# Two fused attention and MLP layers on one core: the opening and the last two tiles rebuilt

## The chip, the core and the metric

The kernel runs on one core of a Trainium2 chip. The metric is the device time of one execution in microseconds (us). Before the change it is 1752.79 us, the median of three runs (1751.76 to 1753.04). The core's engines are named as in the profile: PE (TensorE, matmuls; PEld its weight loads), DVE (VectorE), ACT (ScalarE), POOL (GpSimd) and SP (SyncE, which issues DMAs here). They run side by side, each through its own list of instructions in order, and wait for each other by semaphores.

## The reference

Two times the same pair of layers on 2048 tokens of 512 channels, in bf16, with the same weights in both passes:

```python
def A(x, wqkv, wo):                       # 32 heads of 16 channels
    q, k, v = split(x @ wqkv)
    p = softmax(einsum("bhqd,bhkd->bhqk", q, k) * 16 ** -0.5)
    return merge(einsum("bhqk,bhkd->bhqd", p, v)) @ wo
def B(x, w1, w2):                         # 512 -> 1792 -> 512
    return silu(x @ w1) @ w2
x = x + A(layernorm(x)); x = x + B(layernorm(x))
x = x + A(layernorm(x)); x = x + B(layernorm(x))
```

With 32 heads and 2048 x 2048 scores in each of two layers, the exponentials are the bulk of what has to be done.

## The kernel before, in words

**Tiles.** The 2048 tokens are 16 tiles of 128. A head has 16 channels, so four heads lie side by side in the 128 partitions of a K tile (the `KT` tiles hold keys, transposed, with every other group of 16 partitions set to constants). A *block* is a group of four heads against one chunk of queries: 512 queries, or 256 for the last two chunks of a layer. A *unit* is 512 columns of scores of one head: 128 keys by 512 queries, or two times 128 keys by 256 queries.

**The stream.** `stream` goes through the blocks of both layers. In each step `emit_s` lets PE compute three or two units of scores into one of two PSUM slots (`s3`, 128x1536, and `s2`, 128x1024, in turn), and ACT takes the exp of the whole slot into `p`. Where DVE has room, `spare` gives one more unit to it: it is computed in one of three PSUM banks `g`, and `exp_on_dve` does its exp as a chain of four DVE operations (`v`, then `e` three times). PE then multiplies `p` or `e` by the values (`emit_pv`). A block's sum is copied out of PSUM to `oT`, transposed, and divided by its row sums (`finish_seq`): the transpose is a DMA on SP for most blocks and one on PE for the last two blocks of all (`bank=b in blocks[-2:]`).

**Fill.** All other matmuls (keys, queries, values, projection by `wo`, the two MLP products) are cut into steps of one matmul and put into lanes. `fill_step` puts them into the gaps between scores. `dummy` adds matmuls without use where the planner expects PE to be busy for less than 66% of 3.42 us.

**Who sets the order.** The order is made at build time by a planner in the kernel, `Machine`. It keeps an estimated duration for each instruction and the time at which each engine comes free, tracks which operation reads and writes which stretch of which tile (`span`, `track`), and issues each engine's pending operation that is ready first (`choice`, `pump`); among those, a lower `prio` goes first, and on DVE an operation of `prio` -1 is waited for by up to 0.16 us. PE's order is the order in which `stream` calls it. So every instruction of the listing is recorded at one of a few helper lines: L256 (`Engine.op`, all ACT and DVE operations), L395 (`mm`), L399 (`transpose`), L611 (`by_dma`), L1682 (the dummy exp that loads its table).

**The opening.** After the loads, `x` is normalized (tiles 3 and 7 by sums on ACT, the others by `bn_stats` on DVE), the first eight tiles are scaled into `room` (the `p` tiles), transposed on PE, copied to `xt`, and from these come keys, queries and values of the first block. Along with the first statistics ACT makes eight small constants (`minus`, `extra`, `sel`, 128x4 each), then three groups of roots (`y`), then the dummy exp. A K step (`k_seq`) takes the maximum of |k| (`amaxp`, DVE) and writes two `KT` tiles, one on ACT and one on DVE while nothing streams. A Q step (`q_seq`) makes |q| (`qa`, a DVE operation with a bit mask), a matrix `E` from the maxima and `minus` and `extra`, one matmul `qa` x `E` on top of the queries, and a copy to `qt`. While `before` has work, `order` returns its lanes as `(prep, firsts, turns)` and then `values`.

**The tail.** The last chunk of layer 2 is two tiles. When no scores wait any more, `stream` calls `last` three times: part 0 transposes three quarters of the attention output on PE, and parts 1 and 2 multiply each tile by `wo` into the free score slots, on top of `x` (added by a product with the identity). `end_tokens` then transposes the last quarter, adds its product, runs eight matmuls `warm` without use, copies the two sums to `x_sb` (one on ACT, one on DVE), takes their statistics, makes the reciprocal roots with three Newton steps on DVE for each tile, scales, transposes, runs three more `warm`, then the MLP: 56 matmuls with `w1`, tanh on ACT and a multiply on DVE, 28 matmuls with `w2`, and the sum to `out`.

Of the kernel before, what the change touches and what calls it, by code (L numbers as in the profile page):

```python
# [21 lines left out]
class Op:  # L22
    __slots__ = ("eng", "pitch", "tail", "deps", "end", "fn", "prio")
    __hash__ = object.__hash__

    def __init__(self, eng, pitch, tail, deps, fn, prio):
        self.eng, self.pitch, self.tail, self.deps = eng, pitch, tail, deps
        self.fn, self.prio, self.end = fn, prio, None


class Machine:
# [10 lines left out]
    WINDOW = 3.42  # L42

# [9 lines left out]
    def span(self, ap):  # L53
        key = (ap.name, ap.offset, ap.ap, ap.dtype)
        got = self.cache.get(key)
        if got is None:
            step = ap.ap[0][0]
            lo = ap.offset - ap.start_partition() * step
            hi = lo + 1 + sum(s * (n - 1) for s, n in ap.ap[1:] if s > 0)
            size = BYTES[ap.dtype]  # L60
            g = self.grain.get(ap.name, 1)
            got = self.cache[key] = (lo * size // g, -(-hi * size // g))
        return got

    def track(self, op, reads, writes):
        deps = {}
        for ap in reads:
            lo, hi = self.span(ap)
            known = self.regions.setdefault(ap.name, {})
            for (a, b), (w, _) in known.items():  # L70
                if a < hi and lo < b and w is not None:
                    deps[w] = 1
            mine = known.setdefault((lo, hi), [None, []])
            if op.eng == "PE":
                mine[1][:] = [o for o in mine[1] if o.eng != "PE"]
            mine[1].append(op)
        for ap in writes:
            lo, hi = self.span(ap)
            known = self.regions.setdefault(ap.name, {})
            for (a, b), (w, rs) in list(known.items()):  # L80
                if a < hi and lo < b:
                    if w is not None:
                        deps[w] = 1
                    deps.update(dict.fromkeys(rs))
                    if lo <= a and b <= hi:
                        del known[a, b]
            known[lo, hi] = [op, []]
        deps.pop(op, None)
        return deps

    def written(self, *aps):

        t = 0.0
        for ap in aps:
            lo, hi = self.span(ap)
            for (a, b), (w, _) in self.regions.get(ap.name, {}).items():
                if a < hi and lo < b and w is not None and w.eng != "PE":
# [5 lines left out]
    def released(self, ap):  # L103

        t = 0.0
        lo, hi = self.span(ap)
        for (a, b), (w, rs) in self.regions.get(ap.name, {}).items():
            if a >= hi or lo >= b:
                continue
# [52 lines left out]
    def choice(self, eng):  # L162
# [8 lines left out]
        wait = {-1: 0.16, 0: 0.1} if eng == "DVE" else {}  # L171
# [5 lines left out]

    def pump(self, until):
        while True:
            at, eng = min((self.choice(e)[0], e) for e in self.pending)  # L180
            if at > until:
                return
            at, op = self.choice(eng)
# [138 lines left out]
def kernel(  # L322
# [109 lines left out]
    def best_bank():  # L432
        return min(range(len(banks) if opening[0] else 3), key=bank_time)

    def take_bank():
        i = best_bank()
# [63 lines left out]
    for par in range(2):  # L500
        for out_, i, w in (
            (minus[par][:], 1, 1),
            (extra[par][:], 0, 1),
            (sel[:, par, 0:4], 0, 0),
            (sel[:, par, 4:8], 0, 2),
        ):
            A.activation(
                out_, blk[:], ACT.Identity, scale=cols[:, 2 * par + i, w : w + 1]
            )


# [36 lines left out]
    def ln_stats(mvb, i, tt, **kw):  # L548
        st = st_ring.turn()
        V.bn_stats(st[:], x_sb[:, tt, :], **kw)  # L550
# [137 lines left out]
    def q_seq(L, c, pr, early=False, which=(0, 1), when=None):  # L688
# [3 lines left out]
        def step(ct):  # L692
            def fn(g):
                if ct == 0:
                    box["QT"] = [qt_ring.take() for _ in which]
                    box["E"] = [e_turn[i].turn() for i in range(len(which))]
                    if c == 0:
# [3 lines left out]
                            out=amax[pr][:], in_=amaxp[pr][:, 0:n], axis=AX.X, op=ALU.max  # L701
# [9 lines left out]
                if ct == 0:  # L711
                    for i, par in enumerate(which):
                        V.scalar_tensor_tensor(
                            out=box["E"][i][:, 16 - 16 * par : 128 : 32], in0=minus[par][:],
                            scalar=amax[pr][:, 0:1], in1=extra[par][:], op0=ALU.mult, op1=ALU.add,
                        )
                    if len(which) > 1:
                        V.tensor_scalar_mul(
                            out=box["E"][1][:, 16:128:32], in0=box["E"][0][:, 16:128:32],
                            scalar1=-1.0,  # L720
                        )
                if ct < CT - 1:
                    return
                V.tensor_scalar(
                    out=qa[:].bitcast(U16),
                    in0=g[:, :].bitcast(U16).rearrange("p (n h) -> p n h", h=2)[:, :, 1],
                    scalar1=0x7FFF, scalar2=None, op0=ALU.bitwise_and,
                )
# [56 lines left out]
    def epilogue_seqs(L, c):  # L785
# [12 lines left out]
        def project(i):  # L798
            def step(ct):
                def fn(g):  # L800
# [11 lines left out]
                    ln_stats(box["mvb"], i, tts[i])  # L812
# [14 lines left out]
    def ffn_seqs(L, nxt, c, ln_box):  # L827
# [51 lines left out]
        def down(i):  # L879
            def step(ft):  # L880
                def fn(g):
# [15 lines left out]
                    else:  # L897
                        ln_stats(box["mvb"], i, tts[i])
# [55 lines left out]
    def end_projection(L, box, part, g):  # L954

        attn = L.attn[L.nch - 1]

        aT2 = KT[0][:, 0:1024].rearrange("p (i a b) -> p i a b", i=2, a=CT)  # L960
        if part == 0:
            b = take_bank()
            t_ps = as_bf16(banks[b])[:, 0 : 6 * P].rearrange("p (i a b) -> p i a b", i=2, a=3)
            for i in range(2):
                for ct in range(3):
                    transpose(t_ps[:, i, ct, :], attn[:, i, ct * P : (ct + 1) * P], ident[:, :])
            for i in range(2):
                V.tensor_copy(out=aT2[:, i, 0:3, :], in_=t_ps[:, i])
            give_bank(b)
            box["aT"], box["x"] = aT2, []  # L970
            return
        i = part - 1
        x_ps = s_slots[(g + part) % 2][:, 0, :]
        box["x"].append(x_ps)
        mm(x_ps, lhsT=ident[:, :], rhs=x_sb[:, tiles_of(L, L.nch - 1)[i], :], start=True, stop=False)
        for ct in range(3):
            mm(x_ps, lhsT=aT2[:, i, ct, :], rhs=wo_sb[:, ct, :], start=False, stop=False)

    def end_tokens(L, box, g):

        attn = L.attn[L.nch - 1]
        tts = tiles_of(L, L.nch - 1)
        b = take_bank()
        t_ps = as_bf16(banks[b])[:, 0 : 2 * P].rearrange("p (a b) -> p a b", a=2)
# [3 lines left out]
        give_bank(b)  # L988
        for i in range(2):
            mm(  # L990
                box["x"][i], lhsT=box["aT"][:, i, 3, :], rhs=wo_sb[:, 3, :],
# [8 lines left out]
        for i in (1, 0):  # L1000
            ln_stats(mvb, i, tts[i])
        a, y, ah, t = (keep([P, 2], FP32, f"end{k}") for k in ("a", "y", "h", "t"))
        V.tensor_scalar_add(
            out=a[:].rearrange("p (n o) -> p n o", o=1), in0=mvb[:, 0:2, 1:2], scalar1=float(EPS)
        )
        V.tensor_scalar(
            out=y[:].bitcast(I32), in0=a[:].bitcast(I32), scalar1=-0.5, scalar2=float(0x5F3759DF),
            op0=ALU.mult, op1=ALU.add,
        )
        V.tensor_scalar_mul(out=ah[:], in0=a[:], scalar1=-0.5)  # L1010
        one = [slice(0, 1), slice(1, 2)]
        for _ in range(3):
            for i in one:
                V.scalar_tensor_tensor(
                    out=t[:, i], in0=y[:, i], scalar=ah[:, i], in1=y[:, i],
                    op0=ALU.mult, op1=ALU.mult,
                )
            for i in one:
                V.scalar_tensor_tensor(
                    out=y[:, i], in0=t[:, i], scalar=1.5, in1=y[:, i], op0=ALU.add, op1=ALU.mult  # L1020
                )
        xnT = at_ring.take()[:, :, 0:256]
        for i in range(2):
            V.tensor_scalar(
                out=hT[:, i, :], in0=x_sb[:, tts[i], :], scalar1=mvb[:, i, 0:1], scalar2=y[:, one[i]],
                op0=ALU.subtract, op1=ALU.mult,
            )
        gs = [i for i in range(3) if i != b]
        for i in range(2):
# [3 lines left out]
            dst = xnT[:, :, i * P : (i + 1) * P]  # L1033
# [79 lines left out]
    def stream(layers, before, values, side, last, second_half):  # L1113
# [120 lines left out]
        def emit_s(tp):  # L1234
            g = made[0]
            if not started[0]:
                started[0] = True
                second_half()
# [37 lines left out]
        def finish_seq(b):  # L1276
# [3 lines left out]
            def fn(g):  # L1280
                if c not in L.attn and b.part != "early":
                    L.attn[c] = at_ring.take()
                if g is None:
# [49 lines left out]
                [(fn, b.w, lambda: [oT[:]])], bank=b in blocks[-2:],  # L1333
                when=lambda: b.part == "early" or c in L.attn or at_ring.room(),
            )

        def block_done(b):
# [14 lines left out]
            L.ready[c] = L.ready.get(c, 0) + 1  # L1352
            if L.ready[c] == HB and (c < L.nch - 1 or L.nxt is not None):
# [45 lines left out]
        def step_of(lane, tp, ready=True):  # L1399
# [5 lines left out]
            if s.at == 0:  # L1405
# [4 lines left out]
                if s.bank and bank_time(best_bank()) > (tp + 0.02 if ready else 1e12):  # L1410
# [7 lines left out]
        def do_step(lane):  # L1418
            s = lane.seqs[0]
            if s.at == 0:  # L1420
                if s.lock:
                    Lane.locks.add(s.lock)
                if s.bank:
                    s.own = take_bank()
# [145 lines left out]
        part = 0  # L1570
        while True:
# [13 lines left out]
            if not waiting:  # L1585
                g = made[0] - 1
                if part == 0 and bank_time(best_bank()) <= tp:
                    last(0, g)
                    part = 1
                    continue  # L1590
                if part in (1, 2) and M.released(s_slots[(g + part) % 2][:]) <= tp:
                    last(part, g)
# [203 lines left out]
```

## Time and profile before

| what | us |
|---|---|
| median of three runs | 1752.79 |
| the profiled execution, its own time | 1754.26 |
| its span, from the first instruction to the last event | 1752.4 |
| first exp starts | 22.32 |
| last exp ends | 1722.85 |
| hidden matmuls of the last two tiles start (chain) | 1735.62 |
| waits of ACT between first and last exp, 17 in all | 10.5 |
| exps on ACT: 1536 columns, 1024 columns | 722, 723 |
| exp chains on DVE | 484 |

The page's first part has each engine's busy time and its share of the span. A timeline row has the start and the length in us, the engine, the line of the code, the operation, what it writes and reads and, in brackets, how long its engine was idle before it and for whom it waited. A row of waits has the total in us, the number of waits and the longest. The chain is followed back from the last instruction, each step to what released it.

### The profile page before, as it was taken

The page shows a single profiled execution, that of the slowest core. Times are in us where ns is not written, and L with a number is a line of the kernel's source. Part 1 is how long each engine was busy: PE and PEld are TensorE (multiplying, and loading weights), DVE is VectorE, ACT ScalarE, POOL GpSimd, SP SyncE. Part 2 cuts the span into 40 slices and gives each one's busy share as a digit, 9 for nine tenths or more (in the row PEclk, how much of TensorE's full clock was granted, in tenths as well). Part 3 has the DMA queues.
Part 4 walks back from the last instruction along what each step waited for, and adds up shares of the span by engine and source line. Part 5 has one row for each costly group of instructions (what it writes and reads, how often), then busy time and mean ns, then how long its engine had stood idle before and what let it go on. Part 6 is the DMA issues. An engine that isn't in the chain of part 4 may idle for free.

```text
span 1752.4 us, 32102 instructions
## 1 busy us (share of the span) xinstructions
PE 1532.9 (87%) x12537; PEld 533.0 (30%) x12750; DVE 1640.2 (94%) x3193; ACT 1708.9 (98%) x1604; POOL 6.6 (0%) x20
## 2 busy tenths in 40 slices
PE   8898888898889888898889888889888798888897
PEld 2222222222222223333423222222222222333344
DVE  8999999999989999899899985989999999998995
ACT  8999999999999999999999999999999999999994
POOL 1000000000000000000000000000000000000000
PEclk9998999999999999999999999999999999999999
DMA  5100001000010001000010000100001000110100
GB/s 183 34 10 7 13 19 19 4 19 7 19 16 7 16 7 33 4 16 19 9 23 7 16 7 19 31 7 16 7 16 23 4 19 4 20 18 6 32 12 7
DMA packets 96968, 33.14 MB, mean 19 GB/s; under 512 B 88368, under 2 KB 96304, under 8 KB 96816
## 3 DMA queue, kind: packets, MB, share of 16 engines
q1 hardware_dynamic: 96816, 31.09, 8.0%
q8 instruction: 99, 1.62, 0.4%
q14 instruction: 53, 0.43, 0.1%
HBM read 7.86 MB, written 2.10 MB: 6 GB/s over the span
## 4 chain that ended last, share of the span: by engine, by line
ACT 50%; issue 17%; DVE 16%; PE 14%; DMA 3%; SPq 0%; ACTq 0%; another core or an unknown queue 0%; DVEq 0%
ACT p L256 47%; PE g L395 9%; DVE e L256 6%; PE s L395 5%; DVE v L256 3%; ACT t_sb L256 3%; DMA o<-oT 2%; DVE hT L256 1%; DVE KT L256 1%; DVE amaxp L256 1%; DVE oT L256 0%; DVE qt L256 0%; DVE qa L256 0%; DVE x_sb L256 0%; DMA x_sb<-in_A_x_dram 0%
## 5 line engine op out<-in xcount | busy, mean ns | idle before, releaser
L256 ACT ACTIVATE p<-s 128x1536 bf16<-128x1536 f32 (+1 forms) x1445 | 1664.8, 1397 | 10.1 <-PE s L395 7.6
L395 PE MATMUL s<-qt,KT 32*128 32x512 bf16 (+1 forms) x4513 | 569.0, 338 | 136.0 <-ACT p L256 122.0
L395 PE MATMUL g<-p,vaug 128*32 128x512 bf16 (+1 forms) x4513 | 477.0, 344 | 14.8 <-ACT p L256 13.3
L395 PEld LDWEIGHTS <-KT 32*128 32x128 bf16 x5128 | 209.5, 91 | 651.6 <-issue 639.6
L256 DVE TENSOR_SCALAR v<-g 128x512 f32<-128x512 f32 x484 | 330.6, 683 | 23.1 <-PE g L395 18.0
L256 DVE SCALAR_TENSOR_TENSOR e<-e,v 128x512 uint16<-128x512 bf16 x484 | 327.7, 680 | 0.5
L256 DVE SCALAR_TENSOR_TENSOR e<-v,e 128x512 bf16<-128x512 uint16 x484 | 326.9, 680 | 0.6
L256 DVE SCALAR_TENSOR_TENSOR e<-v 128x512 bf16<-128x512 uint16 x484 | 324.8, 681 | 0.9
L395 PEld LDWEIGHTS <-vaug 128*32 128x32 bf16 x5120 | 139.7, 95 | 210.3 <-issue 197.9
L395 PE MATMUL g<-wo_sb,ident 128*128 128x512 bf16 x612 | 187.7, 384 | 10.7 <-issue 4.0
L395 PE MATMUL g<-qt,KT 32*128 32x512 bf16 (+1 forms) x607 | 187.3, 341 | 0.8 <-DVE hT L256 0.5
L395 PE MATMUL g<-e,vaug 128*32 128x512 bf16 (+1 forms) x607 | 175.8, 345 | 2.7 <-DVE e L256 1.3
L395 PE MATMUL g<-w_sb,hT 128*128 128x512 bf16 x404 | 119.8, 383 | 4.0 <-issue 3.2
L395 PE MATMUL g<-xt,w_sb 128*128 128x512 bf16 x303 | 95.1, 388 | 15.9 <-DVE hT L256 10.1
L256 DVE SCALAR_TENSOR_TENSOR hT<-t_sb,g 128x512 bf16<-128x512 f32 x105 | 71.6, 682 | 17.8 <-ACT t_sb L256 16.7
L395 PEld LDWEIGHTS <-ident 128*128 128x128 bf16 x712 | 54.3, 98 | 101.4 <-issue 81.2
L256 ACT ACTIVATE t_sb<-g 128x512 f32<-128x512 f32 x105 | 77.8, 741 | 0.9 <-PE g L395 0.5
L256 DVE CAST oT<-g 128x512 bf16<-128x512 f32 (+1 forms) x94 | 55.6, 591 | 12.8 <-PE g L395 12.5
L395 PEld LDWEIGHTS <-hT 128*128 128x128 bf16 x568 | 41.5, 97 | 79.9 <-issue 62.5
L395 PEld LDWEIGHTS <-w_sb 128*128 128x128 bf16 x560 | 44.4, 99 | 69.3 <-issue 58.4
L256 DVE CAST qt<-g 128x512 bf16<-128x512 f32 x78 | 53.1, 681 | 3.6 <-PE g L395 3.4
L395 PE MATMUL g<-xt,wq_sb 128*128 128x512 bf16 x141 | 45.1, 393 | 2.8 <-issue 1.9
(129 smaller groups left out, 627.1 us busy)
## 6 DMA issues: line engine op xcount, KB each, us to landing
w_sb<-in_B_w_dram SPq DMA_DIRECT2D x2, 1792.0 KB, 13.9
x_sb<-in_A_x_dram SPq DMA_DIRECT2D x4, 512.0 KB, 6.8
out_dram<-x_sb SPq DMA_DIRECT2D x7, 256.0 KB, 2.1
o<-oT SPq DMA_TRANSPOSE x92, 2.4
xt<-hT SPq DMA_TRANSPOSE x48, 2.4
wk_sb<-in_A_wqkv_dram SPq DMA_DIRECT2D x1, 512.0 KB, 6.0
wq_sb<-in_A_wqkv_dram SPq DMA_DIRECT2D x1, 512.0 KB, 7.0
wv_sb<-in_A_wqkv_dram SPq DMA_DIRECT2D x1, 512.0 KB, 7.9
```

Source lines behind the costliest of these rows:

```text
L256: return self.m.submit(self.name, pitch, tail, aps, outs, lambda: fn(*args, **kw), prio)
L395: lambda: nc.tensor.matmul(out, lhsT=lhsT, rhs=rhs, **kw),
```

## The change: what it does

Opening: the eight constants are submitted after the roots with `prio` 2, so they go where ACT has nothing else; the dummy exp goes behind the first |q|; |q| of the queries made before the first scores is ACT's `Abs` and no longer DVE's bit mask; maxima and `E` get `prio` -1 before the stream starts, and DVE waits up to 0.4 us for such operations until then; the lane of transposes stands ahead of that of keys and queries; a query step takes one of the three `g` banks only.

Stream: the planner tracks a strided tile as up to eight stretches (`spans`) in place of one (`span`), and of two operations at the same time it issues the one that was submitted first.

Tail: three quarters of the last attention output go through two DMA transposes, and the two tiles' first projections become two sequences of fill in the lane `main`, which may begin when `calm` holds (the next-to-last block is done, at most 18 units are left, no DVE chain is under way). They stay in two `g` banks. The next-to-last block's transpose is a DMA; the last block's is put into the slot `s2`. `end_tokens` first runs a dummy square root (table load), takes the statistics of both tiles from PSUM, copies both sums to `x_sb` on ACT, makes one root for both tiles on ACT and one reciprocal on DVE, then a dummy tanh (table load). Both transposed tiles are copied by DVE. `warm` runs eleven and one matmuls in place of eight and three.

The diff, cut to its core:

```diff
 class Machine:
+    WAIT = {-1: 0.16, 0: 0.1}
-    def span(self, ap):
+    def spans(self, ap):
...
+            dims = [(s, n) for s, n in ap.ap[1:] if s > 0 and n > 1]
+            starts = [lo]
+            while len(dims) > 1 and len(starts) * dims[0][1] <= 8:
...
     def pump(self, until):
         while True:
-            at, eng = min((self.choice(e)[0], e) for e in self.pending)
+            at, op = min((self.choice(e) for e in self.pending), key=self.first)
...
                         V.tensor_reduce(
-                            out=amax[pr][:], in_=amaxp[pr][:, 0:n], axis=AX.X, op=ALU.max
+                            out=amax[pr][:], in_=amaxp[pr][:, 0:n], axis=AX.X, op=ALU.max,
+                            prio=0 if started[0] else -1,
                         )
...
-                V.tensor_scalar(
-                    out=qa[:].bitcast(U16),
...
+                if not started[0]:
+                    A.activation(qa[:], g[:, :], ACT.Abs)
+                    if pr == 0:
+                        M.submit(
+                            "ACT", 1.5, 0.1, [qa[:]], [lnt[:, 0:1]],
+                            lambda: nc.scalar.activation(lnt[:, 0:1], onescol[0], ACT.Exp),
+                        )
+                else:
+                    V.tensor_scalar(
...
-    def end_projection(L, box, part, g):
+    def end_projection(L, box, calm):
+        for i in range(2):
+            by_dma(attn[:, i, 0 : 3 * P], aT[:, i, 0:3, :])
...
+            return Seq(
+                [(fn, 512, lambda: [aT[:, i, 0:3, :]]) for fn in steps], bank=False,
+                when=lambda: calm() and bank_time(best_bank()) <= M.now(),
+            )
...
-    def end_tokens(L, box, g):
+    def end_tokens(L, box):
+        first_use(ACT.Sqrt, onescol[0])
...
-        warm(8, idle[:, :])
-        A.copy(x_sb[:, tts[0], :], box["x"][0])
-        V.tensor_copy(out=x_sb[:, tts[1], :], in_=box["x"][1])
+        warm(11, idle[:, :])
...
+        for i in range(2):
+            M.force(V.bn_stats(sts[i][:], x_ps[i]))
+            M.force(A.copy(x_sb[:, tts[i], :], x_ps[i]))
+            give_bank(box["x"][i])
+        for i in range(2):
+            M.force(V.bn_aggr(mvb[:, i, :], sts[i][:]))
+        root, rstd = (keep([P, 2], FP32, n) for n in ("root", "rstd"))
+        A.activation(root[:], mvb[:, 0:2, 1], ACT.Sqrt, bias=eps[:, 0:1])
+        V.reciprocal(rstd[:], root[:])
+        first_use(ACT.Tanh, root[:, 0:1])
...
-            if i == 0:
-                V.tensor_copy(out=dst, in_=t_ps)
-            else:
-                A.copy(dst, t_ps)
-        warm(3, idle[:, :])
+            V.tensor_copy(out=xnT[:, :, i * P : (i + 1) * P], in_=t_ps)
+        warm(1, idle[:, :])
...
+                if b is blocks[-1]:
+                    g = s_slots[1][:, 0, :]
...
-                [(fn, b.w, lambda: [oT[:]])], bank=b in blocks[-2:],
+                [(fn, b.w, lambda: [oT[:]])], bank=False,
...
+        def calm():
+            b = blocks[-1]
+            return blocks[-2].done and sum(b.left) <= GU * DEFER and all(o.end is not None for o in chains)
...
+            if c == L.nch - 1 and L.nxt is None and L.ready[c] == HB - 2:
+                main.add(last(calm))
...
     M.free.update(ACT=4.0, DVE=2.5)
+    M.WAIT = M.WAIT | {-1: 0.4}
...
-        [L1, L2], (prep, firsts, turns), values, side,
-        lambda part, g: end_projection(L2, end_box, part, g), second_half,
+        [L1, L2], (prep, turns, firsts), values, side,
+        lambda calm: end_projection(L2, end_box, calm), second_half,
```

More of the change, by code (lines that the diff above doesn't have):

```diff
@@ L430, in bank_time, with best_bank, take_bank @@
         return INF if shut[i] else M.released(banks[i][:])
[L432 to L436, printed above, removed]
+    def best_bank(every=True):
+        return min(range(len(banks) if opening[0] and every else 3), key=bank_time)
+    def take_bank(every=True):
+        i = best_bank(every)
         assert not shut[i]
@@ L499 @@
     sel = keep([P, 2, 8], BF16, "sel")
[L500 to L509, printed above, removed]
     started = [False]
@@ L1679 @@
     )
[L1680 to L1683 removed]
+    for par in range(2):
+        for out_, i, w in (
+            (minus[par][:], 1, 1),
+            (extra[par][:], 0, 1),
+            (sel[:, par, 0:4], 0, 0),
+            (sel[:, par, 4:8], 0, 2),
+        ):
+            by = cols[:, 2 * par + i, w : w + 1]
+            M.submit(
+                "ACT", 0.12, 0.1, [y[:, 0:1]], [out_],
+                lambda out_=out_, by=by: nc.scalar.activation(out_, blk[:], ACT.Identity, scale=by),
+                prio=2,
+            )
     halves_asked = [True, False]
```

200 lines of the change are left out of this document (95 added, 105 removed).

## The prediction

> **What bounds the kernel now.** I read the engines and the chain first, then ScalarE's waits between the first and the last exp, then the timeline of both ends.
>
> ```profile
> PE 1532.9 (87%) x12537; PEld 533.0 (30%) x12750; DVE 1640.2 (94%) x3193; ACT 1708.9 (98%) x1604; POOL 6.6 (0%) x20
> ...
> ACT 50%; issue 17%; DVE 16%; PE 14%; DMA 3%; SPq 0%; ACTq 0%; another core or an unknown queue 0%; DVEq 0%
> ```
>
> ```profile
> ACT p L256 <- PE s L395: 7.6, 13, 0.9
> ACT p L256 <- PE g L395: 1.9, 4, 0.7
> ```
>
> ScalarE (ACT) bounds: its first exp starts at 22.32, its last ends at 1722.85, and in those 1700.5 us it waits only 10.5 (the five rows of that answer; its two largest are shown). So the time has three terms: 22.32 of opening, the stream (ACT's own work), and a tail of 1752.4 - 1722.85 = 29.55. VectorE's 94% is no bound in the stream: it takes what exps it has room for.
>
> ```profile
> 8.66 0.28 ACT L256 ACTIVATE minus<-blk,cols 128x4 f32<-128x4 f32 x1
> ...
> 10.93 1.28 ACT L1682 ACT_TABLE_LOAD   x1
> 10.94 0.20 DVE L256 RECIPROCAL y<-y 128x8 f32<-128x8 f32 x1 [1.96 <-ACT y L256]
> ...
> 11.96 0.83 PE L399 MATMUL x<-ident,p 128*128 128x128 bf16 x12
> ...
> 16.99 0.69 DVE L256 TENSOR_REDUCE amaxp<-g 128x1 f32<-128x512 f32 x1 [1.40 <-ACT KT L256]
> ...
> 18.91 0.68 DVE L256 TENSOR_SCALAR qa<-g 128x512 uint16<-128x512 uint16 x1
> ...
> 21.00 0.69 DVE L256 CAST qt<-g 128x512 bf16<-128x512 f32 x1 [0.27 <-PE g L395]
> ...
> 22.32 18.27 ACT L256 ACTIVATE p<-s 128x1536 bf16<-128x1536 f32 x16
> ```
>
> In the opening VectorE (DVE) sits 1.96 waiting for ACT's roots, and ACT is late because eight constants stand before them. From 16.99 to 21.69 DVE is busy without a gap worth naming, and the first exp follows its query copy by 22.32 - 21.00 = 1.32.
>
> ```profile
> 1723.48 0.40 PE L395 MATMUL g<-p,vaug 128*32 128x256 bf16 x4
> ...
> 1726.68 0.59 ACT L256 CAST x_sb<-s 128x512 bf16<-128x512 f32 x1 [3.83 <-PE s L395]
> ```
>
> ```profile
> 1735.62 7.25 PE s L395 x56
> 1742.86 0.05 issue
> 1742.91 6.00 PE g L395 x27
> ```
>
> In the tail (timeline, then the chain) every step waits for the one before: the last exp's values product starts 0.63 after it, behind projections, and the 56 hidden matmuls start at 1735.62, 12.77 after it. They take 7.25, because TensorE (PE) has half its clock from 1731 to 1737.8 (windows of 1 us).
>
> **The tail, from the last exp's end at 0.** The change puts both tiles' projections ahead of it as fill, so the product need not queue. Product at 0.06 (PE's usual step after another engine: 1733.67 to 1733.73), 0.40; copy of it 0.50 to 0.92 (0.42); two transposes from 0.98, 0.28; reciprocal 1.30, multiply 1.54 to 1.83, transposes 1.88, copy 2.21, projections 2.56, all at the spacings of the old rows from 1724.68 to 1726.26. First tile's sums 0.42 later, 2.98. DVE now takes statistics straight from PSUM: 2.98 to 3.67 and 3.69 to 4.38 (0.69 each; the reading from PSUM has no row, and I bound it by the same operation's 0.66 and a 512-column PSUM reduce's 0.69). ACT's two copies wait for these, as the order of the instructions shows, 3.70 and 4.41 to 5.00 (0.59). The root is queued behind the second copy: 5.0 to 5.28 (0.28, as the y rows of the opening), reciprocal 5.32 (0.20), two scalings from 5.55, 0.33 apart, transposes 6.02 and 6.54 (0.61), DVE's copies 6.66 and 7.18 to 7.60 (0.42). Hidden matmuls: 7.65 instead of 12.77. What went: 0.87 of queueing, a copy ahead of each statistic, seventeen small DVE operations from 1729.77 to 1733.26, and two of three warming matmuls at half clock (0.43 each). The root's table load (1.28) runs from 0 to 1.5, and the one for tanh from 5.3 to 6.8 with the first tanh due at 9.4: both hidden; beyond these covers each microsecond would count fully.
>
> At full clock the 56 take 6.1 instead of 7.25: 2.23 of the old run was at half clock, which leaves 45.5 matmuls in 5.01, 0.110 each. Then 6.0 down, 0.04, 0.69 and the 2.77 of output as before. The tail is 23.3, 6.25 less.
>
> **The clock takes some back.** In the new tail PE is idle 1.8 of the time from -0.2 to 2.56, as it has no dummies there. The old trace has windows of 3.41 us, with the clock halved in the next one after windows in which PE was 60 to 75% busy or less: six in the stream, but others at 58 to 65% passed. Counted back from the halving at 1730.98, a window that holds over 1.3 us of this idle time starts between -1.65 and 0.7, which is 2.35 of 3.41 positions, 0.7. Then the eleven warming matmuls (2.4) run partly at 0.43, and the transposes wait behind them on PE's queue: 0.5 to 1.05, I take 0.8. So **tail -5.45**.
>
> The Trainium skill (TensorE: Matmul & The Clock Gate, Part 1) has free-running windows of 3413 ns and half clock after at least one idle window. The trace agrees on the length (6.83 us of halving) and not on idle: a window 30% busy was enough. By the page's rule as it stands the tail would be -6.25 and the sum 1746.9.
>
> **The opening.** The constants leave the front of ACT's queue, eight at 0.19 (1.5 with their waits). Roots end at 9.53 instead of 10.91 and DVE's reciprocal starts at 9.56. But PE is in twenty dummies until 11.96 (0.427 each at half clock), so the transposes begin there as before: nothing gained yet. ACT's three copies of transposes run 12.38 to 14.03 (0.53 apart), and one key matmul then stands in PE's queue ahead of the last eight transposes: keys of half 0 end at 15.6 (16.14 before). ACT copies the last tile after four constants, 15.26 to 15.85, which hold it 0.3; keys of half 1 end at 16.9, queries at 17.8. DVE's maximum goes 15.64 to 16.33, ACT's KT 16.36 and 17.10 to 17.88, DVE's KT 17.17 to 17.97 and its second maximum to 18.62; |q| is on ACT, 17.9 to 18.5 (0.59, by the vaug cast), so DVE loses 0.68. amax and E follow, E on PE 19.06, but the second KT (0.80) now stands before the query copy: 20.0. First exp 21.3. The exp table's load, 18.5 to 20.0 with its first use, is under this. **Opening -1.0**, from 0 (the dummies still hold everything) to -2 (their clock rises earlier).
>
> The Trainium skill (ScalarE: Activation LUTs, What ACT_TABLE_LOAD costs) gives 2.66 us a switch, a drain included. Here the load at 10.93 takes 1.28 and its first function runs at 12.22, so no drain shows. By the page the vaug cast after the load would end at 22.0, the opening would win 0.3, and the sum would be 1748.4.
>
> **The stream.** Compared instruction by instruction, DVE does 481 exp chains instead of 484, and ACT one 1536-column exp more. Sixteen exps in 18.27 are 1.14 each; 1536 and 1024 columns differ by 1.609 - 1.186 = 0.42, so a long one is 1.35. **+1.35**. The rest of the order changes too, since the planner tracks strided tiles finely and breaks ties otherwise: ACT's 10.5 of waits may come out from 0 to double. I take no change, by the six half-clock windows there, which hold 4.2 of it (0.7 each): a few windows more or fewer, +-3, is the width. The two DMA transposes added on SP for the projection and the one instead of PE's transpose for the next-to-last block are issued many exps before their users (2.4 to land); no wait.
>
> Sum: -1.0 + 1.35 - 5.45 = -5.1. The profiled run took 1754.26 (span 1752.4 and 1.86 around), so 1749.2 against itself; it stands 1.47 above the median 1752.79, and from that: **1747.7**.
>
> **Rivals.** (1) No halving in the tail: -5.9, 1746.9. For it: the windows at 58 to 65% that passed. (2) The load of the exp table stands in the way, or the dummies do: -4.4, 1748.4. Against it: nothing waits for the load in my order for 1.2 us. (3) The reordered stream loses what the ends win: seven half-clock windows more at 0.7 are +4.9, 1752.6, no change. For it: the windows come where PE is just under its share, which a new order shifts at random. (4) Slower: PE waits in order for things that the planner thinks ready (its costs are written for it), scores queue behind, and ACT waits. An ACT wait costs 0.62 (10.5 over 17); slower by 0.2% needs 8.6, fourteen more among 1445 exps. At twenty more: +7.3, 1760. Against it: the old plan is followed within 17 waits.
>
> **How the numbers follow.** 0.2% is 3.5 us, about what a measurement of this kernel can tell. Forecast 0.42, (1) 0.18, (2) 0.08: faster 0.68; (3) 0.25, same; (4) 0.07, slower. The range goes from the forecast less 4 (no halving, opening -2, stream -2) to the centre of (3): 1743.7 to 1752.8.
>
> **What would show it.** First exp at 21.3; 723 long exps; ACT's waits in the stream near 10; a tail of about 24; hidden matmuls 8.4 after the last exp, at full clock; root right behind the second copy. The prediction is wrong if the stream's waits change by over 3, if the copies do not end before 5.1, or if PE stays at half clock into the hidden matmuls.

## The result and the profile after

Over 20 runs of each, the changed kernel takes 1749.51 us on the median and the kernel before 1754.36; the ratio is 0.9973 (95% interval 0.9962 to 0.9983), 4.7 us less. The profiled execution took 1750.5 (span 1748.7), against 1754.26 (span 1752.4). One run of the kernel before, beside the experiments, took 2166.7 us at a mean granted clock of 0.555; no figure below counts it.

| term | before | forecast | after | forecast of the difference | measured |
|---|---|---|---|---|---|
| first exp starts | 22.32 | 21.3 | 21.49 | -1.0 | -0.83 |
| stream, to the end of the last exp | 1700.53 | 1701.9 | 1703.18 | +1.35 | +2.65 |
| tail | 29.55 | 24.1 | 24.03 | -5.45 | -5.52 |
| span | 1752.4 | 1747.3 | 1748.7 | -5.1 | -3.7 |

The profile's engines and chain of the changed kernel, and ACT's waits from the first exp to the last:

```profile
PE 1575.7 (90%) x12733; PEld 533.1 (30%) x12733; DVE 1629.3 (93%) x3165; ACT 1713.8 (98%) x1610; POOL 6.6 (0%) x20
...
ACT 44%; DVE 21%; PE 16%; issue 15%; DMA 3%; ACTq 0%; DVEq 0%
```

```profile
ACT p L280 <- PE s L419: 7.7, 16, 0.9
ACT p L280 <- PE g L419: 3.1, 5, 1.5
```

ACT is the bound as before. The first of these two rows counts the wait of 0.94 that stands before the first exp and so belongs to the opening. Without it ACT's waits in the stream sum to 10.2 us, against 10.5, so the added 2.65 are no waits that a row shows: they are one long exp more (1.35) and 1.6 besides.

The opening's timeline:

```profile
9.37 0.20 DVE L280 RECIPROCAL y<-y 128x8 f32<-128x8 f32 x1 [0.39 <-ACT y L280]
...
11.79 0.83 PE L423 MATMUL x<-ident,p 128*128 128x128 bf16 x12
...
17.46 0.60 ACT L280 ACTIVATE qa<-g 128x512 bf16<-128x512 f32 x1
18.07 1.28 ACT L743 ACT_TABLE_LOAD   x1
...
19.67 0.68 DVE L280 CAST qt<-g 128x512 bf16<-128x512 f32 x1
...
21.00 0.39 PE L419 MATMUL s<-qt,KT 32*128 32x512 bf16 x3 [0.61 <-DVE vaug L280]
21.49 1.45 ACT L280 ACTIVATE p<-s 128x1536 bf16<-128x1536 f32 x1 [0.94 <-PE s L419]
```

DVE's reciprocal comes 1.57 earlier and waits 0.39 instead of 1.96, yet the first transposes stand where they stood, 11.79 against 11.96. The query copy ends at 20.35, but the first scores wait until 21.00 for another DVE operation, the copy of a values tile (`vaug`): it empties the opening's bank that the first score slot takes over.

The tail's:

```profile
1724.68 1.28 ACT L1014 ACT_TABLE_LOAD   x1
...
1727.93 1.29 DVE L280 BATCH_NORM_STATS2 st<-g 128x6 f32<-128x512 f32 x2 [0.70 <-PE g L419]
1728.12 3.79 PE L419 MATMUL g<-wo_sb,ident 128*128 128x512 bf16 x11
1728.67 1.18 ACT L280 CAST x_sb<-g 128x512 bf16<-128x512 f32 x2 [2.48 <-DVE st L280]
...
1729.74 0.30 ACT L280 ACTIVATE root<-mvb,eps 128x2 f32<-128x2 f32 x1
1730.06 1.28 ACT L1014 ACT_TABLE_LOAD   x1
...
1731.75 0.61 PE L423 MATMUL g<-ident,hT 128*128 128x128 bf16 x8
...
1732.98 6.27 PE L419 MATMUL s<-attn,w_sb 128*128 128x256 bf16 x56 [0.41 <-DVE attn L280]
```

The last exp ends at 1724.66. The root starts 5.08 later, straight behind the second copy, and the first scaled tile is there at about 6.0. The transposes start at 7.09, because eleven warming matmuls stand in front of them and take 3.79: the clock is at half from 1727.2 to 1730.6. The hidden matmuls start 8.32 after the last exp (before: 12.77 by the chain, 12.56 by their timeline row) and run at full clock.

### The profile page after: what moved, and what is told of

It is laid out like the page before. It is cut to its first block, busy times and chain, and to the rows that moved or that the text cites. A ratio compares the mean times of both kernels' runs of the same rounds, so it can differ in the third digit from the quotient of the medians.

```text
span 1748.7 us, 32237 instructions
## 1 busy us (share of the span) xinstructions
PE 1575.7 (90%) x12733; PEld 533.1 (30%) x12733; DVE 1629.3 (93%) x3165; ACT 1713.8 (98%) x1610; POOL 6.6 (0%) x20
## 4 chain that ended last, share of the span: by engine, by line
ACT 44%; DVE 21%; PE 16%; issue 15%; DMA 3%; ACTq 0%; DVEq 0%
ACT p L280 41%; PE g L419 10%; DVE e L280 9%; PE s L419 5%; DVE v L280 4%; ACT t_sb L280 3%; DMA o<-oT 3%; DVE KT L280 2%; DVE hT L280 1%; DVE qt L280 1%; DVE amaxp L280 1%; DVE oT L280 1%; DVE vaug L280 0%; DVE qa L280 0%; DVE attn L280 0%
## 5 line engine op out<-in xcount | busy, mean ns | idle before, releaser
L280 ACT ACTIVATE p<-s 128x1536 bf16<-128x1536 f32 (+1 forms) x1446 | 1671.1, 1410 | 11.7 <-PE s L419 7.7
L419 PE MATMUL g<-wo_sb,ident 128*128 128x512 bf16 x681 | 210.6, 385 | 7.8 <-DVE v L280 5.3
L419 PE MATMUL g<-w_sb,hT 128*128 128x512 bf16 x448 | 131.2, 384 | 0.9 <-DVE hT L280 0.8
L419 PE MATMUL g<-xt,w_sb 128*128 128x512 bf16 x336 | 100.2, 387 | 9.3 <-DVE hT L280 6.5
L280 ACT ACTIVATE t_sb<-g 128x512 f32<-128x512 f32 x105 | 82.4, 784 | 0.6 <-PE g L419 0.3
L419 PE MATMUL g<-xt,wq_sb 128*128 128x512 bf16 x160 | 50.4, 390 | 1.9 <-DVE v L280 0.9
```

What stands on the lines that cost most here:

```text
L280: return self.m.submit(self.name, pitch, tail, aps, outs, lambda: fn(*args, **kw), prio)
L419: lambda: nc.tensor.matmul(out, lhsT=lhsT, rhs=rhs, **kw),
```

## The experiments

My theory is that the three terms add: two ends that win, and a stream that loses through the planner's part. The main rival is that the terms depend on each other: that the fill or the work put off at the ends is paid for in the stream. The table gives one profiled execution of each kernel; "half" is the number of half-clock windows (3.41 us each) within the stream, and ACT's waits are those after the start of the first exp. A ratio is to the runs of before on the same chip, whose median was 1753.8 to 1755.0.

| kernel | median, ratio to before (95%) | first transposes, first exp | stream | long exps, chains | ACT's waits, half | tail |
|---|---|---|---|---|---|---|
| before | 1754.36 | 11.96, 22.32 | 1700.53 | 722, 484 | 10.5, 6 | 29.55 |
| changed | 1749.51, 0.9973 (0.9962 to 0.9983) | 11.79, 21.49 | 1703.18 | 723, 481 | 10.2, 5 | 24.03 |
| changed_again | 1750.53, 0.9983 (0.9970 to 0.9995) | 10.51, 20.21 | 1705.80 | 723, 481 | 13.2, 7 | 22.89 |
| planner_only | 1756.34, 1.0002 (0.9988 to 1.0016) | 12.29, 24.16 | 1701.40 | 723, 480 | 10.3, 3 | 29.04 |
| tail_only | 1751.96, 0.9990 (0.9977 to 1.0003) | 11.83, 23.65 | 1703.14 | 723, 480 | 11.6, 4 | 22.91 |
| open_only | 1760.50, 1.0026 (1.0010 to 1.0042) | 11.74, 21.44 | 1706.95 | 723, 481 | 13.5, 6 | 29.81 |
| old_planner | 1743.96, 0.9941 (0.9925 to 0.9956) | 10.62, 19.87 | 1700.00 | 722, 484 | 9.5, 9 | 23.03 |
| tail_alone | 1749.87, 0.9974 (0.9961 to 0.9988) | 11.85, 22.34 | 1704.66 | 722, 484 | 12.8, 8 | 24.20 |
| gaps_filled | 1749.47, 0.9980 (0.9968 to 0.9992) | 10.77, 20.47 | 1700.60 | 723, 481 | 8.0, 3 | 23.03 |
| warm5 | 1752.59, 0.9987 (0.9976 to 0.9997) | 11.04, 20.74 | 1704.10 | 723, 481 | 11.1, 4 | 24.56 |
| newton | 1754.92, 1.0002 (0.9992 to 1.0011) | 12.03, 21.73 | 1707.32 | 723, 481 | 14.0, 7 | 26.65 |
| dummies13 | 1752.79, 0.9990 (0.9975 to 1.0004) | 10.42, 20.67 | 1702.20 | 723, 483 | 11.9, 5 | 22.93 |
| both_best | 1745.08, 0.9948 (0.9928 to 0.9969) | 10.99, 20.25 | 1697.53 | 722, 484 | 8.5, 5 | 23.22 |
| short_dummies | 1742.98, 0.9935 (0.9918 to 0.9953) | 10.11, 19.54 | 1696.84 | 722, 484 | 7.3, 7 | 23.22 |

**How to read it: the runs of one kernel differ by their half-clock windows.** Every run gives its span s and mean granted clock c, and so the number of windows, n = (1 - c) x 2 x s / 3.413 (c has three digits, so n is good to half a window). A straight line through the 20 runs of the changed kernel has 0.99 us per window (n from 2 to 13, spans 1743.4 to 1757.9, correlation 0.90). With one slope and a constant for each kernel, 227 runs of all kernels give 0.91 us per window and leave a scatter of 1.1. At n = 5 the spans are: before 1750.0, planner_only 1755.0, tail_only 1750.7, open_only 1754.2, changed 1747.4 and 1747.7, gaps_filled 1747.9, warm5 1748.6, newton 1750.6, dummies13 1746.8, tail_alone 1744.8, old_planner 1740.1, both_best 1739.9, short_dummies 1738.2. The n of a run counts its tail too: the old tail has two halved windows of its own, the new one none or one, so between kernels of unlike tails some 1.5 us are to be added.

**planner_only** keeps both ends of before:

```diff
-    def span(self, ap):
+    def spans(self, ap):
...
-            at, eng = min((self.choice(e)[0], e) for e in self.pending)
+            at, op = min((self.choice(e) for e in self.pending), key=self.first)
```

> The kernel before with the planner's part of the change alone (strided tiles tracked as several stretches, ties by order of submission; both ends as before). By my theory the loss in the stream comes from this part: ACT does 723 exps of 1536 columns instead of 722 and DVE 480 chains instead of 484, so the stream is 1.4 to 1.8 us longer (plus or minus 3 by half-clock windows), the first exp stays at 22.3 and the tail near 29.5: the time is 1.5 above before. By the rival, in which the lost chains come from the new ends (the fill at the end, the moved constants), this kernel's stream is that of before, 0 us.

The counts of long exps and of chains (before, then planner_only) are as the theory had them, with neither end changed, so the rival falls:

```profile
L256 ACT ACTIVATE p<-s 128x1536 bf16<-128x1536 f32 x722 | 1161.4, 1609 | 8.6 <-PE s L395 6.9 <-PE g L395 1.2
L256 DVE TENSOR_SCALAR v<-g 128x512 f32<-128x512 f32 x484 | 330.6, 683 | 23.1 <-PE g L395 18.0
...
L280 ACT ACTIVATE p<-s 128x1536 bf16<-128x1536 f32 x723 | 1161.7, 1607 | 5.8 <-PE s L419 3.1 <-PE g L419 2.0 <-ACT p L280 0.2
L280 DVE TENSOR_SCALAR v<-g 128x512 f32<-128x512 f32 x480 | 328.1, 684 | 25.2 <-PE g L419 19.8
```

The stream is only 0.87 longer, but with 3 half-clock windows for 6. And the opening, which I had left at 22.3, is 1.8 later. In its timeline DVE's second maximum waits for the second half of the keys, and |q| comes at 21.61 instead of 18.91:

```profile
19.29 0.69 DVE L280 TENSOR_REDUCE amaxp<-g 128x1 f32<-128x512 f32 x1 [0.74 <-PE g L419]
...
21.61 0.68 DVE L280 TENSOR_SCALAR qa<-g 128x512 uint16<-128x512 uint16 x1
...
24.16 1.45 ACT L280 ACTIVATE p<-s 128x1536 bf16<-128x1536 f32 x1
```

In total the planner's part alone changes nothing that can be measured (1.0002): at n = 5 it costs 5.0 us, about 1.8 of them in the opening, but it has fewer windows, 4.9 a run against 8.6.

**tail_only** and **open_only** add one end each to it.

```diff
-        lambda part, g: end_projection(L2, end_box, part, g), second_half,
+        lambda calm: end_projection(L2, end_box, calm), second_half,
```

> The planner's part and the new tail, the opening as before. If the terms add, as my theory has it: first exp 22.3, tail 24.0, stream 1.4 to 1.8 longer than before, in all 4 us below before. By the rival, in which the tail's gain is bought by fill in the last exps, the stream of this kernel is longer than that of the planner's part alone by 1 us or more.

The tail is 22.91 instead of 29.04; the stream is 1.7 longer than in planner_only, which by itself is what the rival asks for. But ACT does the same instructions in the same order in both streams, so that the starts of each can be set side by side: 1.1 of the 1.7 come in the first 50 us, where only tail_only has a half-clock window (at 41.1), and in the last 150 us, which hold the new fill, the difference only moves between 1.6 and 1.9. So the fill is not what lengthens this stream. At n = 5 the new tail brings 4.3, with the windows of the old tail counted out 5.8.

```diff
-                V.tensor_scalar(
-                    out=qa[:].bitcast(U16),
+                if not started[0]:
+                    A.activation(qa[:], g[:, :], ACT.Abs)
```

> The planner's part and the new opening, the tail as before. Theory: first exp 21.5 (0.8 earlier), tail 29.5, stream 1.4 longer, in all 0.5 us above before, not to be told from no change. Rival (what the opening wins is paid back, since work put off there crowds the first exps): the stream is longer by another 0.8 us, and ACT waits in its first 50 us.

The first exp is 2.7 earlier than in planner_only, but at n = 5 only 0.8 remains; the profiled stream is 5.6 longer, 2.7 of it for three windows more. Its median is 4.2 above planner_only's, partly because it has 9.4 windows a run. The rival's price is seen at n = 5, but not its place, and the one long stream does not show it: ACT's order here is the changed kernel's, whose streams are 1700.6 to 1707.3 long in five runs with 3 to 7 windows.

**old_planner** is the changed kernel with the planner of before.

```diff
-    def spans(self, ap):
+    def span(self, ap):
```

> The changed kernel with both ends new and the planner's tracking and ties as before. Theory: 722 long exps and 484 chains again, so the stream is 1.35 us shorter than in the changed kernel, first exp 21.5, tail 24.0: 6 us below before and 1.3 below the changed kernel, within what the half-clock windows of one run shift (about 1 us each). Rival (the finer tracking is worth something to the new ends): the opening or the tail is over 0.5 us longer than in the changed kernel, and nothing is won.

It is 10.4 us below before by the ratio, where the changed kernel is 4.7 below and 6 was expected. 722 and 484 are back; the opening wins 0.45 more, since no values copy stands before the first scores, and its first transposes came 1.2 earlier by the clock. First and last landmarks, to be held against those of the changed kernel above:

```profile
10.62 0.83 PE L407 MATMUL x<-ident,p 128*128 128x128 bf16 x12
...
19.87 1.45 ACT L264 ACTIVATE p<-s 128x1536 bf16<-128x1536 f32 x1 [0.33 <-PE s L403]
```

```profile
1723.09 2.54 PE L403 MATMUL g<-wo_sb,ident 128*128 128x512 bf16 x11
1725.90 0.72 PE L407 MATMUL g<-ident,hT 128*128 128x128 bf16 x8 [0.27 <-DVE hT L264]
...
1727.14 6.27 PE L403 MATMUL s<-attn,w_sb 128*128 128x256 bf16 x56 [0.31 <-DVE attn L264]
```

Here no window of the tail is halved: the eleven matmuls take 2.54, the transposes wait for DVE again, and the hidden matmuls start 7.27 after the last exp (1719.87).

**gaps_filled** and **warm5** test what the halving costs in the changed kernel's tail.

```diff
                 if b is blocks[-1]:
                     g = s_slots[1][:, 0, :]
+                    warm(2, s_slots[0][:, 2, :])
...
+        warm(2, s_slots[0][:, 2, :])
         for i in range(2):
             transpose(t_ps[:, i, :], attn[:, i, 3 * P : 4 * P], ident[:, :])
         V.tensor_copy(out=box["aT"][:, :, 3, :], in_=t_ps)
+        warm(1, s_slots[0][:, 2, :])
```

> The changed kernel with five matmuls without use put into PE's gaps after the last exp (two while the block's sum is copied, two while it is divided, one while the quarter is copied), into a free bank. Theory: PE's share of its 3.4 us window stays above two thirds, the clock is not halved in the tail, the eleven warming matmuls end before the scaled tiles, and the hidden matmuls start 7.6 us after the last exp instead of 8.3: the tail is 0.7 shorter. Rival (the added matmuls stand in front of the transposes on PE's queue): the chain is longer by up to 0.2 at each of three places, and the tail is 0.3 longer.

```diff
-        warm(11, idle[:, :])
+        warm(5, idle[:, :])
```

> The changed kernel with five warming matmuls in place of eleven. Theory (the transposes wait behind eleven matmuls at half clock): with five, PE is free when the first scaled tile is ready, and the transposes start 1.0 us earlier, 6.0 us after the last exp; the hidden matmuls start at 7.6. Rival (the warming pays for itself): PE is idle for over 1 us, the clock is halved again in the hidden matmuls, which take over 7 us, and the tail is longer by 0.5 or more.

With the gaps filled the granted clock is 1.00 throughout, the eleven matmuls take 2.54 and the tail is 23.03, 1.0 less than in the changed kernel's profile. But of the six profiled tails with eleven matmuls, the root on ACT and unfilled gaps, four were not halved either and took 22.9 to 23.0, and over all runs nothing is won (0.9980 of before, and the changed kernel 0.9973). With five matmuls the transposes do start 5.9 after the last exp, as expected, and the hidden matmuls at 7.1; but the clock then falls in them. In warm5's windows the busy times of PE, PEld, DVE, ACT and POOL stand first and the granted clock behind them:

```profile
1732.00:1733.00 1.00, 1.00 (x8) 0.77 (x8) 0.00 (x0) 0.00 (x0) 0.00 (x0) 0.71 0.00 0
1733.00:1735.70 2.70, 2.70 (x14) 1.95 (x13) 0.00 (x0) 0.56 (x1) 0.00 (x0) 0.50 0.00 0
1735.70:1737.00 1.30, 1.30 (x14) 1.13 (x12) 0.81 (x1) 0.46 (x1) 0.00 (x0) 0.95 0.00 0
```

They take 7.94 and the tail 24.56: the rival is right, the warming pays for itself. The runs agree, though less sharply: 1.2 us above the changed kernel at n = 5, with ratios whose intervals overlap.

**newton** takes the root on ACT back, and with it the two table loads of the tail.

```diff
-        A.activation(root[:], mvb[:, 0:2, 1], ACT.Sqrt, bias=eps[:, 0:1])
-        V.reciprocal(rstd[:], root[:])
+        for _ in range(3):
+            for i in one:
+                V.scalar_tensor_tensor(
...
```

> The changed kernel with the reciprocal roots by three Newton steps on DVE, as before, in place of the root on ACT, its reciprocal and the two table loads at the end. Theory: fifteen small DVE operations at 0.2 us stand where 0.6 us of root and reciprocal stood, so the scaling starts about 2.5 us later; of these the warming matmuls hid 1.0, so the tail is 1.5 to 2.5 longer than the changed kernel's. Rival (the table loads and the second copy on ACT eat what the root saves): the tail is equal within 0.3.

Its profile, second tile scaled and transposed:

```profile
1737.28 0.41 DVE L280 TENSOR_SCALAR hT<-x_sb,mvb,endy 128x512 bf16<-128x512 bf16 x1
1737.74 0.56 PE L423 MATMUL g<-ident,hT 128*128 128x128 bf16 x4 [1.34 <-DVE hT L280]
```

The second tile's scaling starts 8.2 after the last exp (1729.05) instead of 5.9, and the clock falls in the hidden matmuls that follow. The tail is 26.65, 2.6 longer than the changed kernel's and a little over what was expected. So the root on ACT is about half of what the tail wins: 2.6 of 5.5 by these profiles, each with a halved window in its tail, and 3.2 at n = 5.

**dummies13** and **short_dummies** test what holds the opening.

```diff
             if not low(tp) or M.written(x_sb[:, 0, :]) > tp:
                 return False
+            if not started[0] and idle_mm[0] >= 13:
+                return False
```

> The changed kernel with at most 13 matmuls without use in the opening in place of 20. Theory: the first transposes wait for PE's twenty dummies, not for the scaled tiles, which are ready at 10.1; with 13 they start at about 10.3 instead of 11.8, and the first exp comes 1.0 to 1.4 us earlier, at 20.2. Rival (the opening is held by ACT's and DVE's copies, or the clock rises later without the dummies): the first exp stays within 0.4 of 21.5 or comes later, with transposes and keys at half clock.

The transposes start at 10.42, as expected, but the plan changes with the dummies (|q| on ACT comes at 17.79, after amax), and the first exp is at 20.67, not 20.2. So the experiment was repeated with the plan kept, in a kernel that has the other gains too. **both_best** is old_planner with the filled gaps, and **short_dummies** is both_best with the last seven dummies cut:

```diff
-            warm(1, banks[i][:, :])
+            ...
+                    lambda: nc.tensor.matmul(
+                        banks[i][:, 0:64], lhsT=ident[:, :], rhs=rhs[:, 0:64], start=True, stop=True
+                    ),
```

> Both new ends, the planner as before, and the five matmuls without use in PE's gaps after the last exp. If the terms add: first exp 9.25 us after the first transposes (at 20 to 21.3, by when the clock rises), stream as before, tail 23.0 every time: 9 to 10 us below before and 5 below the changed kernel. Rival (the earlier run of both ends with the old planner was low by luck with half-clock windows): 6 us below before, 1.3 below the changed kernel.

> The kernel of both new ends with the old planner and filled gaps, and of the opening's twenty matmuls without use the last seven cut to 64 columns (the plan is the same). Theory: the first transposes start at about 10.4 whenever the clock rises, and the first exp 9.25 us later, at 19.7; on the median 0.7 us less than with twenty whole ones. Rival (the clock rises a window later when PE does less): transposes and keys run at half clock, and the first exp comes at 21 or later.

In short_dummies PE is through its dummies at 9.4 and waits for DVE's scaling:

```profile
9.22 0.22 PE L1582 MATMUL x<-x_sb,ident 128*128 128x64 bf16 x2
10.11 1.05 PE L407 MATMUL x<-ident,p 128*128 128x128 bf16 x12 [0.66 <-DVE p L264]
...
19.54 1.45 ACT L264 ACTIVATE p<-s 128x1536 bf16<-128x1536 f32 x1 [0.33 <-PE s L403]
```

The clock rises at 8.0, no later than elsewhere, so the rival does not come. The first exp is at 19.54, the earliest of all. short_dummies has the lowest median, 1742.98, 11 below before and 7.5 below the changed kernel on the same chip; from both_best, at 1745.08, its interval does not part it.

**tail_alone** is before with the new tail and nothing else.

```diff
+            if c == L.nch - 1 and L.nxt is None and L.ready[c] == HB - 2:
+                main.add(last(calm))
```

> The kernel before with the new tail alone, planner and opening as before (722 long exps, 484 chains). If the terms add: first exp as before, stream as before, tail 23.0 without a half-clock window in it and 24.0 with one, against 29.5: 6 us below before. Rival (part of what the new planner costs comes from the fill in the last exps): the stream is 1 us or more above that of before at the same number of half-clock windows, and the gain is 4 us or less.

The tail is 24.20 (halved once, at 1730.7), 5.35 less than before; at n = 5 the kernel is 5.2 below before, with the old tail's windows counted out 6.7. By that the tail is won and nothing lost in the stream. The ratio alone (4.6 us, from 2.1 to 6.8) would not exclude the rival, and the one profiled stream is 4.1 longer with two windows more. Here too ACT's instructions and their order are those of before, and set side by side the two streams part as follows: 1.3 us between 750 and 950 after the first exp, where neither has a halved window; 1.8 across the two windows that only tail_alone has, at 1030.9 and 1044.6; 1.6 across its third, at 1669.2; and 0.7 back at 1591.0, where only before has one. Over the last 50 us, where the new fill stands, it grows by 0.0. So the rival falls: in these traces the fill in the last exps costs nothing.

> The changed kernel once more, on the same chip as the three others of this call. Theory: 4.5 to 5 us below before, and 5 us above the kernel with both ends new and the old planner. Rival (luck): within 1.5 us of that kernel.

Together with both_best and short_dummies on one chip, the changed kernel is 3.0 us below before by the ratio and 5.5 above both_best, and their intervals just fail to overlap (up to 0.9969, and from 0.9970). The low time of the ends with the old planner was not luck: beside the two ends the planner's part takes back half or more of what they win. The terms do not simply add, though. At n = 5 the new opening is worth 0.8 beside the old tail (open_only against planner_only), 3.3 beside the new tail (changed against tail_only) and 4.7 beside the new tail with the old planner (old_planner against tail_alone).

## Why the prediction was right, point by point

**Tail, -5.45 forecast, -5.52 measured.** Step by step the chain held within 0.6: scaling 5.55 forecast, 5.62 in the profile and 5.40 to 5.55 without halving; hidden matmuls 7.65 forecast without halving, 7.1 to 7.3 in the four tails without it; 0.8 for the halving, 1.0 to 1.3 measured (24.03 and 24.20 against 22.89 to 23.03). The prediction called itself wrong if the copies did not end before 5.1; by their row they end at 5.19, but the root starts at 5.08, so nothing waited for that. The transposes did wait behind the warming matmuls at half clock. Mis-sized was the chance of it, 0.7: of six new tails with eleven warming matmuls, the root on ACT and unfilled gaps, two had it. That the profiled tail was one of the two is luck; without the halving the difference would have been about -6.6.

**Opening, -1.0 forecast, -0.83 measured.** That the twenty dummies hold the first transposes was right, and so was the bound of -2 by the phase of the clock: in the six profiled runs with the changed kernel's opening the first exp comes 9.70 after the first transposes each time, and these start at 10.5 where the clock rises at 7.6, and at 12.0 where it rises at 10.7. What my order missed is the values copy on DVE between the query copy and the first scores, 0.65; it was partly made up by a query copy that started at 19.67 and not at 20.0.

**Stream, +1.35 forecast, +2.65 measured.** The long exp is there, and planner_only shows that it comes from the planner. The term that was mis-sized is the rest, which I set to 0 within 3: it is not only scatter. Without their waits the streams with 722 long exps take 1689.0 to 1691.8, and the six with the new planner and the new opening and 723 take 1692.6 to 1693.4, 2.8 us more on the mean (1690.2 and 1693.0), of which the long exp is 1.35. The waits are higher too: 11.7 on the mean in those six, with 5.3 windows, against 9.7 in the five with 722, with 7.0. planner_only and tail_only, with the new planner and the old opening, take 1691.1 and 1691.5 without their waits, so that part comes only where the new planner and the new opening stand together. Rival (3), a reordered stream that loses what the ends win, was thus a real mechanism, but not by its price: it counted half-clock windows, of which the changed kernel has fewer, 5.8 a run against 8.6 (two of these in the old tail).

**The sum, -5.1 forecast, -4.7 by the ratio.** That it came so near is partly luck. At n = 5 the changed kernel is only 2.6 us below before, 4.1 with the windows of the old tail counted out. A stream dearer than forecast by some 2 us (an estimate from the numbers above) was made up by about one window fewer in it, and by the tails that were not halved.

**Rivals.** The table load (2) is not in the way: it ends at 19.35, and ACT then waits 0.39 and 0.94 for others. The Trainium skill (ScalarE: Activation LUTs, What ACT_TABLE_LOAD costs) adds a drain to each switch of tables. The three loads shown above each take 1.28, with the first function at most 0.02 behind, and no run here shows the drain. For (1), the Trainium skill (TensorE: Matmul & The Clock Gate, Part 1) speaks of an idle window. In the 3.41 us before the changed kernel's halving PE was at work for nearly all of the first 0.87 and 0.97 of the last 2.54, so the window need not be idle. PE's waits for a wrong plan (4) did not come: ACT's 10.2 us in the stream are 21 waits. The 10.5 of before are 21 too, with those before tanh; the prediction and the table ahead of it count the 17 before exps. So a wait costs 0.50 and not 0.62, and the twenty more of rival (4) would have come to +4.9 and not +7.3. And 1752.8, the top of the range, is the median of before; the sum of rival (3) is 1752.6.

**What stays open.** Which half of the planner's part, the finer tracking or the order of ties, gives DVE three or four chains fewer was not tried, since all runs change both together; nor was it shown why the new opening is worth so much less with the new planner, and least beside the old tail, or in which stage of the stream it loses part of its gain.

## What to carry to other kernels

Cut the time at two landmarks of the bounding engine, its first and its last long operation, and forecast the three pieces apart: both ends can be followed instruction by instruction, while the middle moves with the plan. Measure each part of a change that has several, and also the whole without it: here the part that looked like bookkeeping changed nothing that could be measured alone, cost 5.6 us beside the two ends, and the ends without it won 10.4. Where two kernels give the bounding engine the same instructions in the same order, set their starts side by side: a difference then has a place. Where runs of one kernel differ, look at the granted clock of each run before its code.

## What the runs showed of the hardware

A half-clock window of 3.41 us goes with 0.9 us more in this kernel (227 runs), though ACT bounds it; set side by side, before and tail_alone part by 0.7 and 1.6 us at a window that only one of them has. The runs of before have 4 to 18 such windows, those of the changed kernel 2 to 13. A window need not be idle to be followed by a halved one: in all 14 traces, from the first exps on, every window in which PE was busy for under 53% of the time was (with matmul ends as the profile models them), and busier ones went either way. The clock of the opening, read from the starts of PE's matmuls without use (0.43 us apart, then 0.21), rises between 7.6 and 10.7 us after the span's start in runs of the same instructions, by which the first exp moves by 1.5 us. Statistics of 512 columns straight from PSUM take as long as from SBUF: two in 1.29, from PSUM and from SBUF.
